# Splitting the last 512-token block of a fused attention/FFN/soft-MoE kernel in two, sharing its regrouping transfers between two queues, and moving one accumulator update

## The chip, the cores and the metric

The kernel runs on one core of a Trainium2 chip. The metric is the device time of the kernel in microseconds (us). A core has TensorE (PE, matrix products; PEld is its loading of stationary operands), VectorE (DVE), ScalarE (ACT) and GpSimd (POOL). SyncE (SP) computes nothing; in this kernel it issues nearly all DMA transfers. Every engine works through its own instructions in order.

## The reference

```python
kv = einsum('bhsd,bhse->bhde', k, v)              # 8 batches, 8 heads, 576 tokens, head size 64
out = einsum('bhsd,bhde->bhse', q, kv)
out = out / sqrt(mean(out*out, -1) + 1e-6) * g_norm        # -> x: 4608 tokens x 512
h = x @ w_in ; g = h * cos(h) ; y = g @ w_out              # w_in 512 x 2048, w_out 2048 x 512
logits = y @ phi                                           # 32 slots (8 experts x 4)
d = softmax of logits over the tokens ; slot_input = d.T @ y
slot_out[e] = relu(slot_input[e] @ w1[e]) @ w2[e]          # w1, w2: 8 x 512 x 1024, 8 x 1024 x 512
result = softmax(logits over the slots) @ slot_out         # 4608 x 512
```

All is float32. `y` is never formed: the kernel folds `w_out` into `phi` (`wp`) for the logits, and accumulates `A = d.T @ g` over the tokens with a running maximum, to multiply it by `w_out` once at the end.

## The kernel before

Tokens come in nine blocks `j` of 512 (`TB`). A block has 16 slots `f`, one for each 128 of the 2048 columns of `w_in`. A slot `(j, f)` runs in this order: `loads` (DMA issues planned for it), `main` (12 matmuls into PSUM tile `h`, of which there are three), `side` (planned work of other stages), `cos_a` (ACT turns `h` into turns, DVE takes the rest, L387), `post`, `cos_b` (ACT cosine, L391), `cos_c` (DVE multiplies, L437, giving `gT`; then a DVE 32x32 transpose into `tr`, L446), and `fin`. Tables name the slot at which each side task runs; a slot number over 15 is in the next block.

The side tasks that matter here:
- `att_out`, `att_xs`, `att_xT`, `att_lo` make the next block's `xt` (split in two parts) from `q` and the block-diagonal `kvA`. `att_out` ends with a small power on POOL (`ri`, L214), which `att_xs` on DVE needs one slot later.
- `load_kv` (L162) loads pair 0 to 3 of a batch in slots 10 to 13; `kv_pair` (L183, tile `kvps`) uses pairs 0 and 1 in slot 14, 2 and 3 in slot 18.
- `nat_load`, `nat_scale`, `nat_bits`, `nat_low`, `nat_store` (L333, L338, L352) convert `w_out` in blocks 3 to 6 and put it into DRAM as `wo_dr`, by way of the tiles that the kv loads use.
- `regroup` (L480): `tr` holds tokens scattered over partitions by the 32x32 transposes; sixteen transfers of 64 KB for each group of four slots bring them into `g` with tokens on partitions. They stand in slots 7 and 8, 9 and 10, 13 and 14, 17 and 18. All are issued by SP, in one queue with every other load; only the last block has every other one on POOL. Blocks 0, half of 1 and half of the last use transposes on PE instead (`gtr`, L462).
- `l_T` and `slot_acc` (slots 21 and 22, which are 5 and 6 of the next block): 16 matmuls `ab<-g,d` (L588), then on DVE at once `A = A*mb + ab` (L591).

The queue of SP (and that of POOL) has eight semaphores, used in turn, so a transfer is issued only after the eighth before it has landed.

When a buffer is free for good, `fill` loads expert weights (33.5 MB in 128 pieces of 256 KB) into it, in the order in which the tail uses them: `kv`, `vr`, `kr` from slot (7,8), `q`, `kvA` from (7,13), `a` at (8,0), `x1` (8 pieces) at (8,2), `T2` at (8,4), then the weight tiles as the last block uses them up. `load_wo2` loads the converted `w_out` (4.2 MB) in slots 1 to 8 of the last block. All others (84 pieces) come behind the last block. `last_product` computes the last slot in two halves. `last_slots`, then `tail`: `first_layer` (L734), `second_layer` (L761), `half_out` (L786, L788) with twelve 768 KB stores.

Of the kernel before, what the change touches and what calls it, by code (L numbers as in the profile page):

```python
# [50 lines left out]
    lT=21,  # L51
# [14 lines left out]
TB, TT, NB, NR = 512, 4, 9, 6  # L66
# [3 lines left out]
def tile_linear_attention__ffn_cos__soft_moe(  # L70
# [70 lines left out]
    def spans(j, t):  # L141
        p, r = divmod(TT * j + t, 9)
        if r == 4:
            return [(0, 64, 2 * p), (64, 64, 2 * p + 1)]
        return [(0, 128, 2 * p + r // 5)]

    def load_q(j, t):
        if j == 0:
            if t == 0:
                first["q"] = g_p.tile([128, TT, 4, 128], F32, tag="g1", name="q")  # L150
            q_t[j, t] = first["q"][:, t]
        else:
            q_t[j, t] = q_p.tile([128, 4, 128], F32, tag=f"q{(TT * j + t) % 3}", name="q")
        nc.sync.dma_start(out=q_t[j, t], in_=qT[TT * j + t])
# [105 lines left out]
    def stage():  # L260
        ta, tb, tc_ = (t_p.tile([128, 2048], F32, tag=f"T{i}", name="st") for i in range(3))
        wi = const.tile([128, 2, 512], F32, tag="l_tok", name="st_m")
        first["sx"] = x_p.tile([128, 2 * TT, 512], F32, tag="x1", name="st_x")
# [3 lines left out]
        ring.extend([None, ta[:, TB * i:TB * (i + 1)], 1] for i in range(3))  # L267
# [92 lines left out]
    def main(j, f, s=slice(0, TB), ps=None):  # L360
        if ps is None:
            ps = ps_m.tile([128, 512], F32, tag="h", name="h")[:, 0:s.stop - s.start]
        w, x = w_t[f], xt_t[j]
        assert all((j, t) in x_done for t in range(TT)) and ("S", f, 0) in done
        n = 0
        for kk in range(KD):
            for a, b in ((0, 0), (0, 1), (1, 0)):
                nc.tensor.matmul(out=ps, lhsT=w[:, a, kk, :], rhs=x[:, b, kk, s],  # L368
# [38 lines left out]
    def last_product(j, f):  # L407
        ss = [slice(0, TB // 2), slice(TB // 2, TB)]
        hs, ts = [], []
        for i, s in enumerate(ss):  # L410
            main(j, f, s, at_bank("h2")[:, 0:TB // 2] if i else None)
            hs.append(h_t.pop((j, f)))
        run(side, j, f)
        for h in hs:
            ts.append(tmp_one()[:, 0:TB // 2])
            turns(ts[-1], h)
            rest(ts[-1], h)
        run(post, j, f)
        g = ring_next(j, f)
        for t in ts:  # L420
            cosine(t)
        for s, h, t in zip(ss, hs, ts):
            nc.vector.tensor_tensor(out=g[:, s], in0=t, in1=h, op=ALU.mult)
        gT_t[j, f] = g
        run(fin, j, f)

    def ring_next(j, f):
        i = next(i for i, r in enumerate(ring) if (r[0] not in gT_t or j == NB - 1)
                 and (not r[2] or j == 0 or j == 1 and f < 10))
        _, g, extra = ring.pop(i)  # L430
        ring.append([(j, f), g, extra])
        return g

    def cos_c(j, f):
# [4 lines left out]
        if not on_pe(j, f):  # L439
            q, o = divmod(f, 4)  # L440
            if o == 0:
                k = 4 * j + q - 5
                tr_t[j, q] = t_p.tile([128, 4 * TT, 4, 32], F32, tag=f"T{k % 3}", name="tr")
            first_o = 2 if (j, q) == (1, 2) else 0
            for i in range(0 if o == first_o else o, o + 1 if o >= first_o else 0):
                nc.vector.transpose(out=tr_t[j, q][:, :, i, :],  # L446
                                    in_=gT_t[j, 4 * q + i].rearrange("p (b t) -> p b t", t=32))

    def g_half(j, h):
        if (j, h) not in g_t:  # L450
            if (j, h) == (1, 0):
                g_t[j, h] = [x.rearrange("p (x f i) -> p x f i", f=8, i=32) for x in
                             (kv_all[:, 0], kv_all[:, 1], kv_all[:, 2], we)]
            else:
                t = g_p.tile([128, TT, 4, 8, 32], F32, tag=f"g{h}", name="g")
                g_t[j, h] = [t[:, i] for i in range(TT)] + [t]
        return g_t[j, h]

    def gtr(j, f):
        ps = at_bank("tr").rearrange("p (t c) -> p t c", c=128)  # L460
        for t in range(TT):
# [4 lines left out]
        if len(g) > TT:  # L466
            copy_on(e, g[TT][:, :, :, f % 8, :], p4)
# [41 lines left out]
    def l_evac(j):  # L509
        t = one_p.tile([128, TB], F32, tag="ls", name="ls")  # L510
# [629 lines left out]
```

## Time and profile before

| | |
|---|---|
| median of 3 runs | 747.95 us (747.94 to 752.03) |
| profiled execution | 751.21 us, of which span 749.4 us |
| PE / PEld busy | 687.2 us (92%) / 490.7 us (65%) |
| DVE / ACT / POOL busy | 500.7 us (67%) / 333.1 us (44%) / 103.9 us (14%) |
| granted TensorE clock, mean | 0.961 of full speed |
| DMA | 135.09 MB, 58.5% of 16 engines on SP's queue |
| chain that ended last | PE 43%, DMA 21%, SP's queue 14%, DVE 12% |

Shares are shares of the span. The chain follows the last instruction back to what released it. A PE that is busy 92% on average can still be waiting in some stretches and held by DMA in others, so the stretches are read apart: the blocks (180 to 600 us), the last block (600 to 660) and the tail.

### The profile page before, as it was taken

The page shows a single profiled execution, that of the slowest core. Times are in us where ns is not written, and L with a number is a line of the kernel's source. Part 1 is how long each engine was busy: PE and PEld are TensorE (multiplying, and loading weights), DVE is VectorE, ACT ScalarE, POOL GpSimd, SP SyncE. Part 2 cuts the span into 40 slices and gives each one's busy share as a digit, 9 for nine tenths or more (in the row PEclk, how much of TensorE's full clock was granted, in tenths as well). Part 3 has the DMA queues.
Part 4 walks back from the last instruction along what each step waited for, and adds up shares of the span by engine and source line. Part 5 has one row for each costly group of instructions (what it writes and reads, how often), then busy time and mean ns, then how long its engine had stood idle before and what let it go on. Part 6 is the DMA issues. An engine that isn't in the chain of part 4 may idle for free.

```text
span 749.4 us, 11987 instructions
## 1 busy us (share of the span) xinstructions
PE 687.2 (92%) x4432; PEld 490.7 (65%) x4432; DVE 500.7 (67%) x884; ACT 333.1 (44%) x600; POOL 103.9 (14%) x121
## 2 busy tenths in 40 slices
PE   6869999999979999879987997899999999999894
PEld 6757777876637776567656765677676775764354
DVE  4986888866638778747874787577877875443143
ACT  3655676545414453425343534354454443441143
POOL 3351121210000111000100010011001102201400
PEclk9888999999989999989998999899999999999996
DMA  9872543121254745556555456545542778999998
GB/s 335 307 243 89 188 150 117 67 85 43 59 135 100 191 136 126 143 162 160 132 143 161 129 137 156 149 125 140 123 100 62 195 196 255 268 333 418 402 406 347
DMA packets 96058, 135.09 MB, mean 180 GB/s; under 512 B 10880, under 2 KB 66304, under 8 KB 95104
## 3 DMA queue, kind: packets, MB, share of 16 engines
q1 hardware_dynamic: 95488, 133.28, 58.5%
q0 software_dynamic: 512, 1.05, 0.5%
q8 instruction: 35, 0.57, 0.3%
q14 instruction: 23, 0.19, 0.1%
HBM read 91.29 MB, written 13.63 MB: 140 GB/s over the span
## 4 chain that ended last, share of the span: by engine, by line
PE 43%; DMA 21%; SPq 14%; DVE 12%; issue 4%; ACT 3%; POOL 0%; DVEq 0%; ACTq 0%; POOLq 0%
PE h L368 25%; SPq L480 12%; DMA ew<-in_w 7%; DMA kv<-in_w_out 6%; PE ab L588 4%; DMA kv<-in_kv 2%; DVE gT L437 2%; DVE tmp L387 2%; ACT tmp L391 2%; DVE tr L446 2%; PE ops L202 2%; PE tr L462 2%; PE xTps L232 2%; PE kvps L183 2%; DMA q<-in_qT 1%
## 5 line engine op out<-in xcount | busy, mean ns | idle before, releaser
L368 PE MATMUL h<-xt,w 128*128 128x512 f32 (+1 forms) x1740 | 424.3, 398 | 9.4 <-DVE gT L437 6.8
L368 PEld LDWEIGHTS h<-xt,w 128*128 128x128 f32 x1740 | 322.1, 190 | 103.0 <-issue 18.3
L391 ACT ACTIVATE tmp<-tmp,hpi 128x512 f32<-128x512 f32 (+1 forms) x145 | 104.3, 721 | 177.6 <-DVE tmp L387 177.5
L437 DVE TENSOR_TENSOR gT<-tmp,h 128x512 f32<-128x512 f32 x135 | 92.6, 686 | 69.6 <-ACT tmp L391 69.2
L214 POOL TENSOR_TENSOR ri<-ss,mhalf 128x8 f32<-128x8 f32 x36 | 59.4, 1654 | 428.7 <-DVE ss L212 428.7
L387 DVE SCALAR_TENSOR_TENSOR tmp<-h,tmp 128x512 f32<-128x512 f32 (+1 forms) x145 | 97.3, 671 | 29.7 <-ACT tmp L384 28.8
L384 ACT ACTIVATE tmp<-h 128x512 int32<-128x512 f32 (+1 forms) x145 | 85.1, 588 | 48.7 <-PE h L368 48.7
L446 DVE STREAM_TRANSPOSE tr<-gT 128x512 f32<-128x512 f32 x112 | 79.4, 711 | 3.8
L588 PE MATMUL ab<-g,d 128*32 128x512 f32 x240 | 39.5, 615 | 6.3 <-DMA g<-tr 5.2
L236 ACT ACTIVATE xt<-xTps,gn 128x512 fp32r<-128x512 f32 x36 | 24.6, 682 | 45.7 <-PE xTps L232 45.7
L202 PE MATMUL ops<-kvA,q 128*128 128x128 f32 (+1 forms) x320 | 38.8, 280 | 0.0
L183 PE MATMUL kvps<-kv 128*64 128x64 f32 x464 | 20.5, 236 | 18.9 <-issue 11.0
L202 PEld LDWEIGHTS ops<-kvA,q 128*128 128x128 f32 (+1 forms) x320 | 34.7, 182 | 3.1 <-issue 1.5
L183 PEld LDWEIGHTS kvps<-kv 128*64 128x64 f32 x464 | 17.2, 146 | 29.0 <-issue 25.4
L245 DVE SCALAR_TENSOR_TENSOR xt<-xTps,gn,xt 128x512 fp32r<-128x512 f32 x36 | 26.6, 739 | 13.9 <-ACT xt L236 13.8
L588 PEld LDWEIGHTS ab<-g,d 128*32 128x32 f32 x240 | 11.6, 112 | 33.3 <-issue 25.8
L311 POOL TENSOR_TENSOR w<-st_m,w 128x512 fp32r<-128x512 f32 x16 | 21.6, 1348 | 78.5 <-ACT w L306 74.5
L209 ACT ACTIVATE sq<-ops 128x512 f32<-128x512 f32 x32 | 19.1, 596 | 27.9 <-PE ops L202 27.7
L211 DVE TENSOR_REDUCE ss<-sq 128x8 f32<-128x512 f32 x32 | 21.8, 680 | 12.6 <-ACT sq L209 12.5
L492 PE MATMUL l<-gT,wp 128*32 128x512 f32 x216 | 28.8, 605 | 0.0
L232 PE MATMUL xTps<-ident,sq 128*128 128x128 f32 x128 | 23.0, 312 | 1.1 <-DVE sq L221 1.1
L221 DVE TENSOR_TENSOR sq<-ops,ri 128x512 f32<-128x512 f32 x32 | 21.5, 678 | 2.4 <-POOL ri L214 2.4
(160 smaller groups left out, 637.7 us busy)
## 6 DMA issues: line engine op xcount, KB each, us to landing
g<-tr SPq DMA_DIRECT2D x432, 64.0 KB, 2.1
kv<-in_kv SPq DMA_DIRECT2D x29, 512.0 KB, 5.3
ew<-in_w SPq DMA_DIRECT2D x27, 512.0 KB, 12.5
q<-in_qT SPq DMA_DIRECT2D x36, 256.0 KB, 3.1
out<-ot SPq DMA_DIRECT2D x12, 768.0 KB, 6.6
rw<-in_w_in SPq DMA_DIRECT2D x16, 512.0 KB, 5.8
kv<-in_w_out SPq DMA_DIRECT2D x16, 512.0 KB, 3.6
st<-in_w_outT SPq DMA_DIRECT2D x15, 512.0 KB, 3.8
```

Of the source, the lines that this page charges most:

```text
L183: nc.tensor.matmul(out=ps[h], lhsT=t[:, 0, r, h], rhs=t[:, 1, r, h], start=(r == 0), stop=False)
L202: nc.tensor.matmul(out=ps[p0:p0 + n, pr * 128:(pr + 1) * 128], lhsT=q_t[j, t][:, pr, p0:p0 + n], rhs=kvbd[b % 2][:, pr, :], start=True, st ...
L214: nc.gpsimd.tensor_tensor(out=ri[:, :, 0], in0=ss, in1=mhalf, op=ALU.pow)
L232: nc.tensor.transpose(ps[:, kk * 128:(kk + 1) * 128], xs[:, kk * 128:(kk + 1) * 128], ident)
L368: nc.tensor.matmul(out=ps, lhsT=w[:, a, kk, :], rhs=x[:, b, kk, s], start=(n == 0), stop=(n == 3 * KD - 1))
L384: nc.scalar.activation(out=t.bitcast(I32), in_=ps, func=AF.Copy, bias=0.25, scale=INV_2PI)
L387: nc.vector.scalar_tensor_tensor(out=t, in0=ps, scalar=INV_2PI, in1=t.bitcast(I32), op0=ALU.mult, op1=ALU.subtract)
L391: nc.scalar.activation(out=t, in_=t, func=AF.Sin, bias=hpi, scale=TWO_PI)
L437: nc.vector.tensor_tensor(out=g, in0=fr, in1=h_t.pop((j, f)), op=ALU.mult)
L446: nc.vector.transpose(out=tr_t[j, q][:, :, i, :], in_=gT_t[j, 4 * q + i].rearrange("p (b t) -> p b t", t=32))
L480: (nc.gpsimd if j == NB - 1 and b % 2 else nc.sync).dma_start(out=dst[32 * b:32 * b + 32, :, x, a:a + 4, :].rearrange("p t f i -> p t (f i)"),
L588: nc.tensor.matmul(out=ps[32 * c:32 * c + 32, :], lhsT=d[:, t, :], rhs=gs[c // 2][t][:, (c % 2) * 512:(c % 2) * 512 + 512], start=(t == 0) ...
```

## The change

1. The nine blocks of 512 become eight of 512 and two of 256 (`SIZES`; `SMALL` is 8, the first of the small ones). Every tile of a block takes its size from the list. The small blocks use eight slots to one regrouping group (1 KB runs where there were 512 bytes), one `g` tile for both halves, halves of the old `gT` ring, and halves of one `tmp`. The last block's `xt` lies in `T2`. The regrouping of a small block stands in slots 9 and 10, 17 and 18; the last one's second half is still transposed on PE. `last_product` is gone.
2. `ring` and `tmp` are two tiles each, so that one of each can be freed early. The fills move: `x1` to (8,1), `gt1` and `tmp1` at (8,5), `q` and `kvA` to (8,12), `a` to (8,15), `x0` at (9,0), `load_wo2` to block 9, `T1` at (9,6), `g0` at (9,12), `T0` at (9,14). Before the end of the last block 68 pieces are issued instead of 44.
3. Every other regrouping transfer is issued by POOL in all blocks.
4. The update of `A` becomes `slot_add`, planned in `fin` of the slot instead of directly behind the matmuls.

```diff
-TB, TT, NB, NR = 512, 4, 9, 6
+TB = 512
+SIZES = (512,) * 8 + (256,) * 2
...
+SMALL = SIZES.index(256)
...
         for x in xs:
             for b in range(4):
-                (nc.gpsimd if j == NB - 1 and b % 2 else nc.sync).dma_start(
-                    out=dst[32 * b:32 * b + 32, :, x, a:a + 4, :].rearrange("p t f i -> p t (f i)"),
+                (nc.gpsimd if b % 2 else nc.sync).dma_start(
+                    out=dst[32 * b:32 * b + 32, :, x, a:a + n, :].rearrange("p t f i -> p t (f i)"),
...
+        ab_t[j] = (ps, mb)
+
+    def slot_add(j):
+        if j == NB - 1:
+            return
+        ps, mb = ab_t.pop(j)
         if j:
             nc.vector.scalar_tensor_tensor(out=A, in0=A, scalar=mb[:, 3:4], in1=ps,
                                            op0=ALU.mult, op1=ALU.add)
...
+        lT, sa = (PLAN["F"][j] if j < 2 else (22, 23) if j == NB - 1 else (23, 26) if j >= SMALL
+                  else (PLAN["lT"], PLAN["sa"]))
         at2(j, lT, l_T, j)
         at2(j, sa, slot_acc, j)
+        end2(j, sa, slot_add, j)
...
+    ld_at(8, 1, fill, x_p, "x1", 8)
+    ld_at(8, 5, fill, gt_p, "gt1", 3)
+    ld_at(8, 5, fill, const, "tmp1", 1)
...
+    ld_at(9, 0, fill, x_p, "x0", 8)
     for n in range(8):
-        ld_at(8, n + 1, load_wo2, n)
-    ld_at(8, 4, fill, t_p, "T2", 4)
+        ld_at(9, n + 1, load_wo2, n)
+    ld_at(9, 6, fill, t_p, "T1", 4)
+    ld_at(9, 12, fill, g_p, "g0", 8)
+    ld_at(9, 14, fill, t_p, "T0", 4)
```

SP's order in block 3, from the issue behind slot 6 on (`kv<-in_w_out` is nat_load, `wo_dr<-kv` nat_store, `kv<-in_kv` load_kv), before:

```order
L333 DMA kv<-in_w_out 128x1024
L480 DMA g<-tr 32x4x128 x8
L352 DMA wo_dr<-kv 4x32x512
L333 DMA kv<-in_w_out 128x1024
L480 DMA g<-tr 32x4x128 x16
L154 DMA q<-in_qT 128x512
L480 DMA g<-tr 32x4x128 x8
L162 DMA kv<-in_kv 128x1024
L352 DMA wo_dr<-kv 4x32x512
L162 DMA kv<-in_kv 128x1024
```

and now:

```order
L340 DMA kv<-in_w_out 128x1024
L476 DMA g<-tr 32x4x128 x4
L359 DMA wo_dr<-kv 4x32x512
L340 DMA kv<-in_w_out 128x1024
L476 DMA g<-tr 32x4x128 x8
L160 DMA q<-in_qT 128x512
L476 DMA g<-tr 32x4x128 x4
L168 DMA kv<-in_kv 128x1024
L359 DMA wo_dr<-kv 4x32x512
L168 DMA kv<-in_kv 128x1024
```

The order is the same; between the slot-6 issue and the second pair's load stand 16 regrouping transfers instead of 32.

DVE in slots 5 to 7 of the same block, around the update of `A` (L591 before), before:

```order
L446 STREAM_TRANSPOSE tr<-gT 128x16x32
L300 SCALAR_TENSOR_TENSOR kv<-kv 128x512
L591 SCALAR_TENSOR_TENSOR A<-A,mb,ab 128x512
L245 SCALAR_TENSOR_TENSOR xt<-xTps,gn,xt 128x4x128
L387 SCALAR_TENSOR_TENSOR tmp<-h,tmp 128x512
L221 TENSOR_TENSOR sq<-ops,ri 128x512
L437 TENSOR_TENSOR gT<-tmp,h 128x512
L446 STREAM_TRANSPOSE tr<-gT 128x16x32
L387 SCALAR_TENSOR_TENSOR tmp<-h,tmp 128x512
```

and now (L594):

```order
L437 STREAM_TRANSPOSE tr<-gT 128x16x32
L307 SCALAR_TENSOR_TENSOR kv<-kv 128x512
L252 SCALAR_TENSOR_TENSOR xt<-xTps,gn,xt 128x4x128
L393 SCALAR_TENSOR_TENSOR tmp<-h,tmp 128x512
L227 TENSOR_TENSOR sq<-ops,ri 128x512
L427 TENSOR_TENSOR gT<-tmp,h 128x512
L437 STREAM_TRANSPOSE tr<-gT 128x16x32
L594 SCALAR_TENSOR_TENSOR A<-A,mb,ab 128x512
L393 SCALAR_TENSOR_TENSOR tmp<-h,tmp 128x512
```

The update, which waits for the matmuls on PE, now stands behind the whole of slot 6 on DVE.

SP from the last group of block 7 on (`ew` are expert weights, `wo` is load_wo2), before, where that is in the last block:

```order
L480 DMA g<-tr 32x4x128 x8
L643 DMA ew<-in_w 128x512 x2
L480 DMA g<-tr 32x4x128 x8
L945 DMA wo_5244<-wo_dr 128x1024
L480 DMA g<-tr 32x4x128 x8
L643 DMA ew<-in_w 128x1024
L643 DMA ew<-in_w 128x2048
```

and now, in the first small block:

```order
L476 DMA g<-tr 32x4x128 x12
L646 DMA ew<-in_w 128x512
L646 DMA ew<-in_w 128x2048
L646 DMA ew<-in_w 128x1536
L476 DMA g<-tr 32x4x128 x4
L646 DMA ew<-in_w 128x512
L646 DMA ew<-in_w 128x1024
L646 DMA ew<-in_w 128x512
L476 DMA g<-tr 32x2x256 x8
```

The eight pieces of `x1` (4096 columns) now stand ahead of the last four transfers of block 7 on SP; the other eight of that group are on POOL.

## Rows read from the trace of the kernel before

**Rows 1.** Windows: stretch, engines' busy us, then granted clock, DMA share, GB/s

```profile
194.50:204.50 10.00, 10.00 (x57) 7.58 (x54) 6.39 (x17) 5.25 (x9) 1.64 (x1) 1.00 0.44 93
...
323.60:340.00 16.40, 16.40 (x112) 12.95 (x114) 10.03 (x17) 5.87 (x9) 0.00 (x0) 0.85 0.51 132
...
598.20:656.70 58.50, 57.51 (x285) 40.50 (x282) 32.93 (x55) 27.34 (x44) 8.97 (x16) 1.00 0.85 237
...
680.40:715.90 35.50, 33.00 (x280) 11.00 (x279) 9.06 (x12) 4.59 (x7) 9.77 (x36) 1.00 1.03 408
```

**Rows 2.** Waits of the whole span: total us, times, longest

```profile
DVE A L591 <- PE ab L588: 15.1, 7, 10.0
...
PE kvps L183 <- issue: 11.0, 2, 5.6
...
PE h L368 <- DVE gT L437: 6.8, 9, 1.2
```

**Rows 3.** Timeline of PE around kv_pair: start, us, instruction, [idle before]

```profile
251.45 0.64 PE L183 MATMUL kvps<-kv 128*64 128x64 f32 x16
...
252.54 11.16 PE L368 MATMUL h<-xt,w 128*128 128x512 f32 x48
...
323.57 1.12 PE L183 MATMUL kvps<-kv 128*64 128x64 f32 x16 [5.49 <-DMA kv<-in_kv]
...
325.61 12.48 PE L368 MATMUL h<-xt,w 128*128 128x512 f32 x48
```

**Rows 4.** Timeline of SP's queue: start, us, issues

```profile
194.25 10.39 SPq L480 DMA_DIRECT2D g<-tr  x16
...
286.07 6.40 SPq L480 DMA_DIRECT2D g<-tr  x8
...
293.69 13.56 SPq L480 DMA_DIRECT2D g<-tr  x16
...
313.14 0.52 SPq L162 DMA_DIRECT2D kv<-in_kv  x1
...
314.39 0.40 SPq L162 DMA_DIRECT2D kv<-in_kv  x1
```

**Rows 5.** Timeline of PE around slot_acc, of block 1 and of block 2

```profile
211.24 1.03 PE L588 MATMUL ab<-kv,d 128*32 128x512 f32 x4
...
218.03 1.03 PE L588 MATMUL ab<-g,d 128*32 128x512 f32 x1 [4.14 <-DMA g<-tr]
...
223.87 5.74 PE L368 MATMUL h<-xt,w 128*128 128x512 f32 x24
...
282.12 4.72 PE L588 MATMUL ab<-g,d 128*32 128x512 f32 x32 [0.27 <-DVE d L564]
```

**Rows 6.** Timeline of POOL: its first regrouping issues in the last block

```profile
629.75 3.99 POOL L480 DMA_DIRECT2D g<-tr  x7 [37.78 <-DMA ew<-in_w]
636.29 0.56 POOL L480 DMA_DIRECT2D g<-tr  x1 [2.55 <-DMA g<-tr]
```

**Rows 7.** L480 on POOL: from issue to landing of its transfers

```profile
DMA to landing us min/median/max: 5.8/6.7/7.2
```

**Rows 8.** Groups by form, those of 256 columns: busy us, mean ns | idle before

```profile
L368 PE MATMUL h<-xt,w 128*128 128x256 f32 x24 | 3.1, 287 | 0.0
...
L391 ACT ACTIVATE tmp<-tmp,hpi 128x256 f32<-128x256 f32 x2 | 0.9, 500 | 0.2 <-DVE tmp L387 0.2
...
L387 DVE SCALAR_TENSOR_TENSOR tmp<-h,tmp 128x256 f32<-128x256 f32 x2 | 0.8, 420 | 1.6 <-ACT tmp L384 1.6
```

**Rows 9.** Timeline of PE in the tail

```profile
668.54 2.16 PE L608 MATMUL ab<-g,d 128*32 128x128 f32 x64 [0.58 <-DVE d L564]
...
705.78 0.59 PE L761 MATMUL eo<-kv,hT 128*32 128x256 f32 x2
...
715.88 1.21 PE L772 MATMUL sel<-so,sel 128*96 128x256 f32 x4
...
720.29 1.50 PE L761 MATMUL eo<-ew,hT 128*32 128x256 f32 x24
```

More of the change, by code (lines that the diff above doesn't have):

```diff
@@ L65 @@
 )
-TB, TT, NB, NR = 512, 4, 9, 6
+TB = 512
+SIZES = (512,) * 8 + (256,) * 2
+NB = len(SIZES)
+TT = [n // 128 for n in SIZES]
+T0 = [sum(TT[:j]) for j in range(NB)]
+NT = sum(TT)
+SMALL = SIZES.index(256)
 @with_exitstack
@@ L357, in on_pe, with main @@
         return j == 0 or j == 1 and f < NF // 2 or j == NB - 1 and f >= NF // 2
-    def main(j, f, s=slice(0, TB), ps=None):
-        if ps is None:
-            ps = ps_m.tile([128, 512], F32, tag="h", name="h")[:, 0:s.stop - s.start]
+    def main(j, f):
+        ps = ps_m.tile([128, 512], F32, tag="h", name="h")[:, 0:SIZES[j]]
         w, x = w_t[f], xt_t[j]
-        assert all((j, t) in x_done for t in range(TT)) and ("S", f, 0) in done
+        assert all((j, t) in x_done for t in range(TT[j])) and ("S", f, 0) in done
         n = 0
@@ L405, in cos_b @@
         cosine(fr_t[j, f])
[L407 to L425, printed above, removed]
     def ring_next(j, f):
+        if (j, f) == (SMALL, 0):
+            ring[:] = [[r[0], r[1][:, a:a + 256], 2 * r[3], r[3]] for k in range(2) for r in ring
+                       if r[3] == k and r[2] != 1 for a in (0, 256)]
         i = next(i for i, r in enumerate(ring) if (r[0] not in gT_t or j == NB - 1)
[L429 to L432, printed above, removed]
+                 and (not r[2] or r[2] == 1 and (j == 0 or j == 1 and f < 10) or r[2] == 2 and (j, f) < (SMALL, 2)))
+        r = ring.pop(i)
+        ring.append([(j, f)] + r[1:])
+        return r[1]
     def cos_c(j, f):
@@ L555, in l_exp @@
         sc_t[j] = mb
+    ab_t = {}
     def l_T(j):
@@ L604, in ab @@
             ps = abs_[o % 2]
-            for t in range(TT):
+            for t in range(TT[-1]):
                 for c in range(4):
@@ L678, in c_split @@
         if j not in cs_t:
-            w = w_p.tile([128, 3, 3, 3 * NS], F32, tag=f"w{10 + j // 3}", name="cs")
-            cs_t.update((j + x, w[:, x]) for x in range(3))
+            w = x_p.tile([128, 12, 3, 3 * NS], F32, tag="x1", name="cs")
+            cs_t.update((x, w[:, x]) for x in range(12))
         cs = cs_t[j]
@@ L813, in tail @@
         second_layer(1, 1)
-        half = {1: (select(1), two(g_p, "g1") + two(g_p, "g0") + two(gt_p, "gt"))}
+        half = {1: (select(1), two(g_p, "g0") + [gt_p.tile([128, 1536], F32, tag=f"gt{i}", name="ot") for i in (1, 0)]
+                    + two(g_p, "g1"))}
         for u in range(2):
@@ L921, in tile_linear_attention__ffn_cos__soft_moe @@
             ao, dx, xt, dl = PLAN["A"][n]
-        for t in range(TT):
-            i = TT * j + t + 3
-            if i < TT * NB:
-                ld_at(n, ao[t] + 1, load_q, *divmod(i, TT))
+        for t in range(TT[j]):
+            i = T0[j] + t + 3
+            if i < NT:
+                jj = max(x for x in range(NB) if T0[x] <= i)
+                ld_at(n, ao[t] + 1, load_q, jj, i - T0[jj])
             at2(n, ao[t], att_out, j, t)
```

154 lines of the change are left out of this document (80 added, 74 removed).

## The prediction

> **What bounds the kernel now.** I read the windows by stage first. PE runs nearly without a break in the blocks, and from the last block on the DMA engines are the fuller resource: their share is 0.85 while the last block is computed and 1.03 at 408 GB/s in the tail [rows 1]. So two questions: what holds PE in the blocks, and what holds DMA in the tail.
>
> The list of waits answers the first. PE's dearest waits are not for another engine but for a load: the second pair of `kv_pair` waits 5.49 us in block 3 [rows 3], and two more, of up to 5.6 us, 11.0 together, are booked as "issue" in blocks 4 and 5 [rows 2]; the timeline puts them at the same matmul. The load is not slow because of its size. It is issued at 314.39 [rows 4], some nine microseconds before PE resumes at 323.57 [rows 3], because SP stands behind regrouping transfers: from 286.07 SP issues 8 and then 16 and 8 more of them, and comes to the kv loads at 313.14 [rows 4]. The price goes on after the wait: from the late pair to the end of the next 48 matmuls PE takes 338.09 - 323.57 = 14.52 us, against 263.70 - 251.45 = 12.25 for the same work in block 2 [rows 3]; the granted clock in that stretch is 0.85 [rows 1], a mixture of the two levels, after an idle PE. One wait thus costs 5.5 + 2.3 us.
>
> The same queue holds the accumulation of block 1: `ab` begins at 211.24, stops 4.14 us for a regrouping transfer, and the next main product begins at 223.87, 12.6 us later; the same 32 matmuls take 4.72 us in block 2 [rows 5]. In the tail the second layer's first half of experts 4 to 7 begins at 705.78 and ends at 715.88, 10.1 us for 64 matmuls of which 24 take 1.50 us elsewhere, that is 4.0 us [rows 9]: the weights come late.
>
> **POOL takes half of the regrouping.** SP issues 16 transfers in 10.39 us, 0.65 each [rows 4]. Between the issue behind slot 6 and the second kv load stand 32, now 16: that load can be issued up to 16 x 0.65 = 10.4 us earlier, and 5.5 are needed. It also waits for the conversion of `w_out` to leave its buffer, but that conversion's own load stands behind the same transfers and moves up too. The DMA engines have room: with SP issuing nothing but regrouping their share is 0.44 [rows 1], so two queues ask for about 0.88. I take the three waits as gone: 11.0 + 5.5 + 3 x 2.3 = 23.4 us. Bounds: nothing gained if the load lands as late as now, 23.4 at most.
>
> A rule speaks against this. The Trainium skill, "DMA: Bandwidth & Descriptors", section "Issuing engines are not separate DMA queues", says that transfers started from several engines share the same 16 DMA engines, and that starting them from more than one saves only sequencer time, usually small beside the transfer. By the rule's "usually" the term would be near 0; by the row it is 23.4, since the sequencer needs 0.65 us for a transfer and the engines are only 0.44 busy meanwhile.
>
> Block 1's `ab`: SP's 32 transfers ahead of it become 16, 10 us less for a 4 us wait. 12.6 - 4.7 = 7.9; I take 7.5 (bounds 4.1, the wait alone, and 7.9).
>
> POOL has its own price. It issued seven transfers in 3.99 us (0.57 each), and the eighth waited 2.55 us, until the first had landed [rows 6], 6.7 us after its issue [rows 7]. That was with DMA full; at that pace 16 transfers need about 0.85 us each, 14 us, in blocks of over 60 us. Behind them on POOL stands `ri`, for which DVE's `att_xs` waits. Eight transfers (4.6 us at 0.57) begin when `ab` ends, in slot 6, and the next `ri` belongs to slot 8: hidden, 0.
>
> **The update of `A` moves.** DVE waited 15.1 us for `ab` in seven places, 10.0 of them in block 1 [rows 2], with slot 6's rest queued behind. Now the slot's cosine runs under the matmuls, and what is late next is the next slot's rest, by less. PE gets back part of its 6.8 us of waits for `gT` [rows 2]; bounds 0 and 6.8, I take 2. Against it: while PE waited for kv, DVE and ACT caught up. Without those breaks new short waits of PE may come; bounds 0 and 8 (those 6.8 once more and a little), I take 3, about half.
>
> Blocks together: -23.4 - 7.5 - 2 + 3 = -29.9 us.
>
> **Two small blocks.** 24 products of 256 columns take 3.1 us [rows 8], so a slot 1.55; 32 slots 49.6. Before, 15 slots of 12 x 11.16/48 = 2.79 us [rows 3] and the split one of 3.1 made 45.0. So +4.6. One more accumulation with two token tiles instead of four, half of 4.72: +2.4. Further logits, max and transposes for one more block, less the narrower PE transposes: +1, my estimate from the counts of instructions, of the length of one such group. DVE and ACT alternate in a slot: rest 420 ns, cosine 500 ns [rows 8], multiply and transpose each about as long as the rest: 1.76 us against 1.55 on PE, in 24 slots up to 5 us, of which accumulations and attention on PE hide a good half: +2 (bounds 0 and 9, if fixed costs and the softmax's short steps show). Together +10.
>
> The last group of block 7 must land before `ab` in slot (8,6), and before ACT may write `xt` into `T2` at (8,5). Its last four on SP stand behind `x1`, 2.1 MB, 5.1 us at 408 GB/s; its eight on POOL need 8 x 0.57 + 6.7 = 11.3 us. Slots of 1.55 us and a few others give about 11 to 14 us: +2, bounds 0 and 6.
>
> **The tail.** `last_slots` has half the matmuls; 64 take 2.16 us [rows 9], 64 of 128 go: -2.2. Maximum, exponential and copies of half size: -1 (0 to 2). The late second layer: 24 more pieces, 6.3 MB, are issued before the last block ends, 15.4 us at 408 GB/s. Room for them: 0.15 of 58.5 us is 8.8 us [rows 1], and the longer small blocks add about 12. So they fit and 10.1 - 4.0 = 6.1 us go (bounds 0 and 6.1). The rest, from 715.88 [rows 9] to the span's end 749.4, is 33.5 us for 9.4 MB of output, 23 us at 408 GB/s, partly shared with weights now: -2 (0 to 6). Together -11.3.
>
> **Sum.** -29.9 + 10 + 2 - 11.3 = -29.2 on the profiled execution's 751.2 us gives 722.0; that execution is 3.3 us above the median of 747.95, so 718.8 by the median. I say 718.5.
>
> **Rivals.**
> - The kv waits close only in part, because two queues fill the DMA engines in bursts and each transfer lands later (6.7 us on POOL when full [rows 7]). For it: the kv load took nine microseconds though the DMA engines were about half busy (0.51 in the stretch behind it [rows 1]). With 10 of 23.4 us gained, 732.
> - The end costs more: small slots paced by DVE and ACT (+17 instead of +10), the last group of block 7 late (+6), weights not earlier (-5 instead of -11.3): 17 more, 736. Against it: DMA room worked out above.
> - No effect: the 16 engines, not the issue, set the pace. Then only -2 and +3 remain in the blocks, and the end's +0.7: 750 by the median. Against it: share 0.44 [rows 1].
> - Slower: POOL's issues are held. Place: eight issues between the end of `ab` in slot 6 and `ri` of slot 8. From there to `att_xs` are about 16 us in block 3, less 1.6 for `ri`: above some 1.8 us an issue, against 0.57 measured, DVE and then PE wait. At 3 us they wait 10 us in each of five blocks: 718.5 + 50 = 768. The Trainium skill, "SBUF — State Buffer", section "SBUF: two separate sides", gives such a mechanism: DVE in a two-port mode keeps POOL from writing its descriptors. No run here shows it; the only POOL issues [rows 6] lie where the conversion of `w_out` does not run.
> - Better: DMA never falls behind, outputs follow at once, no new DVE waits: 706.
>
> **How the numbers follow.** Forecast 0.58 (its own range 709 to 728), partly closed 0.13, dear end 0.13, no effect 0.05, slower 0.06, better 0.05. The range 704 to 738 takes in all but the "no effect" and "slower" cases and the edges of the dear end. About 1% (7.5 us) is what a measurement of this kernel can tell from no change; below 740.5 lie the forecast, better and most of the two dear cases: faster 0.88, same 0.06, slower 0.06.
>
> **What would show it.** Right: no wait over 1 us at `kvps` in blocks 3 to 5; `ab` of block 1 near 4.7 us; SP's kv loads before slot 12; blocks 8 and 9 about 10 us longer than block 8 was; the second layer without DMA waits. Wrong: `att_xs` waiting for `ri`, PE waiting for `g<-tr` in block 8, a DMA share at 1.0 already in blocks 3 to 6, or small slots near 2 us.

## The result, and the profile after

The changed kernel takes 724.21 us (median of four executions, 718.57 to 726.98) against 749.99 us for the kernel before on the same chip: a ratio of 0.964, 95% interval 0.955 to 0.972. The prediction was 718.5 us with a range of 704 to 738. The profiled execution took 718.57 us (span 716.6); it is the quickest of its four, and the experiments show what probably separates them.

The time went as follows. Stages are cut at PE rows: where the accumulation `ab` of blocks 0 and 6 begins (slot 6 of blocks 1 and 7), the end of the last `main`, the first product of the first expert layer (`eh`), the first `sel`. The column in the middle is experiment e1, explained below: the kernel before with nothing but POOL's half of the regrouping.

| stage, us | before | e1 | after |
|---|---|---|---|
| start to `ab` of block 0 | 190.5 | 190.4 | 190.1 |
| to `ab` of block 6 | 375.6 | 340.1 | 340.3 |
| to the end of the last `main` | 93.7 | 92.9 | 108.8 |
| last softmax, slot inputs | 20.6 | 20.7 | 16.0 |
| first layer, half of the second | 35.5 | 27.9 | 27.9 |
| output | 33.5 | 32.5 | 33.4 |
| span | 749.4 | 704.5 | 716.6 |

The changed kernel is better than before by 33 us of span in these two profiles, and worse than one of its own parts by 12. Windows of it, columns as in [rows 1]:

```profile
274.20:339.50 65.30, 63.50 (x390) 45.91 (x390) 51.63 (x96) 29.98 (x49) 24.38 (x36) 1.00 0.64 170
...
530.50:639.30 108.80, 101.56 (x706) 79.72 (x703) 70.27 (x157) 50.16 (x103) 35.45 (x59) 0.98 0.78 227
...
655.30:683.20 27.90, 27.88 (x279) 10.35 (x278) 8.98 (x11) 4.59 (x7) 9.76 (x36) 1.00 1.03 399
```

From `ab` of block 2 to `ab` of block 3 it takes 65.3 us, PE busy in 63.5 of them at a granted clock of 1.00; before it took 356.51 - 282.12 = 74.4. The DMA share is 0.64, so the 16 engines are not full.

PE at `kv_pair` in block 3, to be held against [rows 3]: the long wait is gone, and the 48 products behind it are back at the full clock.

```profile
308.69 0.64 PE L189 MATMUL kvps<-kv 128*64 128x64 f32 x16
...
309.78 11.16 PE L374 MATMUL h<-xt,w 128*128 128x512 f32 x48
```

SP's queue ahead of it, to be held against [rows 4]: 4, 8 and 4 transfers stand where 8, 16 and 8 stood. The second load leaves at 297.75, 10.9 us before PE comes to the pair at 308.69; before, 318.08 - 314.39 = 3.7 us (323.57 less the wait of 5.49). The lead grew by 7.2 us where 5.5 were missing.

```profile
278.33 2.86 SPq L476 DMA_DIRECT2D g<-tr  x4
...
282.94 9.88 SPq L476 DMA_DIRECT2D g<-tr  x8
...
293.50 2.54 SPq L476 DMA_DIRECT2D g<-tr  x4
...
296.15 0.52 SPq L168 DMA_DIRECT2D kv<-in_kv  x1
...
297.75 0.33 SPq L168 DMA_DIRECT2D kv<-in_kv  x1
```

POOL at the place that the prediction named, between the end of `ab` in slot 6 and the next `ri`: seven issues, a hold of 1.01 us, the eighth issue, then an idle engine until `ss` is there. Here `ri` waits for its input, and not for the issues ahead of it.

```profile
278.71 4.04 POOL L476 DMA_DIRECT2D g<-tr  x7 [1.88 <-PE ab L585]
283.76 0.55 POOL L476 DMA_DIRECT2D g<-tr  x1 [1.01 <-issue]
287.76 1.67 POOL L220 TENSOR_TENSOR ri<-ss,mhalf 128x8 f32<-128x8 f32 x1 [3.46 <-DVE ss L218]
```

Block 1's `ab`, [rows 5] before, runs through; the next `main` starts 215.88 - 210.87 = 5.0 us after it begins, where it was 12.6.

```profile
210.87 0.62 PE L585 MATMUL ab<-kv,d 128*32 128x512 f32 x2
...
215.88 0.97 PE L374 MATMUL h<-xt,w 128*128 128x512 f32 x3
```

The two small blocks, PE. Two long waits are new, for `ld` of the softmax and for `gT` right behind a softmax step. `ab` of block 7 starts without a wait. The first half of the second layer, [rows 9] before, now runs from 676.22 to 683.24 with no wait for weights.

```profile
577.49 0.46 PE L559 MATMUL ldT<-ident,ld 64*128 64x64 f32 x4 [2.43 <-DVE ld L542]
...
581.64 5.09 PE L585 MATMUL ab<-g,d 128*32 128x512 f32 x32
...
600.95 6.65 PE L374 MATMUL h<-xt,w 128*128 128x256 f32 x48
...
617.41 2.93 PE L374 MATMUL h<-xt,w 128*128 128x256 f32 x12 [3.24 <-DVE gT L427]
...
676.22 3.64 PE L764 MATMUL eo<-ew,hT 128*32 128x512 f32 x32
...
683.24 1.23 PE L775 MATMUL sel<-so,sel 128*96 128x256 f32 x4
```

DVE in four small slots without other work. The rest of one slot begins 1.79 us after that of the slot before (602.68 - 600.89, 604.47 - 602.68), and each multiply has waited 0.58 us for ACT's cosine: DVE goes through rest, wait, multiply, transpose in strict order.

```profile
600.89 0.39 DVE L393 SCALAR_TENSOR_TENSOR tmp<-h,tmp 128x256 f32<-128x256 f32 x1
...
602.68 0.39 DVE L393 SCALAR_TENSOR_TENSOR tmp<-h,tmp 128x256 f32<-128x256 f32 x1
603.64 0.42 DVE L427 TENSOR_TENSOR gT<-tmp,h 128x256 f32<-128x256 f32 x1 [0.58 <-ACT tmp L397]
604.10 0.45 DVE L437 STREAM_TRANSPOSE tr<-gT 128x256 f32<-128x256 f32 x1
604.47 0.38 DVE L393 SCALAR_TENSOR_TENSOR tmp<-h,tmp 128x256 f32<-128x256 f32 x1
```

### The profile page after: what moved, and what is told of

The parts are those of the page before. It is cut to its first block, busy times and chain, and to the rows that moved or that the text cites. A ratio compares the mean times of both kernels' runs of the same rounds, so it can differ in the third digit from the quotient of the medians.

```text
span 716.6 us, 12698 instructions
## 1 busy us (share of the span) xinstructions
PE 673.7 (94%) x4578; PEld 492.2 (69%) x4578; DVE 509.6 (71%) x941; ACT 339.0 (47%) x635; POOL 225.7 (32%) x337
## 4 chain that ended last, share of the span: by engine, by line
PE 58%; DVE 18%; DMA 10%; ACT 7%; issue 4%; SPq 1%; POOL 0%; DVEq 0%; ACTq 0%; POOLq 0%
PE h L374 35%; DMA kv<-in_w_out 4%; PE ab L585 4%; DVE gT L427 4%; ACT tmp L397 3%; DVE tmp L393 3%; PE ops L208 3%; DVE tr L437 2%; PE l L488 2%; PE kvps L189 2%; PE eh L737 2%; DVE ss L217 2%; PE tr L457 2%; PE xTps L239 2%; PE l L497 1%
## 5 line engine op out<-in xcount | busy, mean ns | idle before, releaser
L374 PEld LDWEIGHTS h<-xt,w 128*128 128x128 f32 x1920 | 332.7, 190 | 99.3 <-issue 18.3
L397 ACT ACTIVATE tmp<-tmp,hpi 128x512 f32<-128x512 f32 (+1 forms) x160 | 108.8, 681 | 172.5 <-DVE tmp L393 172.4
L476 POOL DMA_DIRECT2D g<-tr x232 | 128.3, 556 | 115.4 <-DVE tr L437 45.6
L427 DVE TENSOR_TENSOR gT<-tmp,h 128x512 f32<-128x512 f32 (+1 forms) x152 | 95.8, 630 | 77.8 <-ACT tmp L397 77.4
L390 ACT ACTIVATE tmp<-h 128x512 int32<-128x512 f32 (+1 forms) x160 | 87.5, 547 | 54.8 <-PE h L374 53.8
L437 DVE STREAM_TRANSPOSE tr<-gT 128x512 f32<-128x512 f32 (+1 forms) x128 | 84.4, 661 | 6.0 <-DMA g<-tr 0.5
L318 POOL TENSOR_TENSOR w<-st_m,w 128x512 fp32r<-128x512 f32 x16 | 23.7, 1479 | 77.4 <-ACT w L313 77.4
L488 PE MATMUL l<-gT,wp 128*32 128x512 f32 (+1 forms) x248 | 30.2, 559 | 0.0
L239 PE MATMUL xTps<-ident,sq 128*128 128x128 f32 x128 | 20.5, 287 | 0.4 <-DVE sq L227 0.4
```

Of the source, the lines that this page charges most:

```text
L390: nc.scalar.activation(out=t.bitcast(I32), in_=ps, func=AF.Copy, bias=0.25, scale=INV_2PI)
L397: nc.scalar.activation(out=t, in_=t, func=AF.Sin, bias=hpi, scale=TWO_PI)
L427: nc.vector.tensor_tensor(out=g, in0=fr, in1=h_t.pop((j, f)), op=ALU.mult)
L437: nc.vector.transpose(out=tr_t[j, q][:, :, i, :], in_=gT_t[j, n * q + i].rearrange("p (b t) -> p b t", t=32))
L476: (nc.gpsimd if b % 2 else nc.sync).dma_start(out=dst[32 * b:32 * b + 32, :, x, a:a + n, :].rearrange("p t f i -> p t (f i)"), in_=src[32 ...
L488: nc.tensor.matmul(out=l_t[j][32 * o:32 * o + 32, :], lhsT=wp[:, f, :], rhs=gT_t.pop((j, f)), start=(c == 0), stop=(c == (2 if j == NB - 1 ...
```

## The experiments

Each was run in four executions beside the kernel before on the same chip; e3 had ten. Parts are numbered as in the text: 1 the two small blocks, 2 the half-size buffers and the loads moved with them, 3 POOL's half of the regrouping, 4 the update of `A`.

### e1: part 3 alone

```diff
-                (nc.gpsimd if j == NB - 1 and b % 2 else nc.sync).dma_start(
+                (nc.gpsimd if b % 2 else nc.sync).dma_start(
```

> The kernel before with one edit: every second regrouping transfer is issued by POOL in all blocks (part 3 alone). My theory (the three long waits at `kv_pair` are the place of the kv loads in SP's queue behind 16 transfers of 0.65 us each): no wait over 1 us at `kvps` in blocks 3 to 5, the `ab` of block 1 at 4.7 to 6 us where it was 13 us with its 4.14 us wait, the starts of `ab` in blocks 3, 4 and 5 earlier by 16 to 18, 26 and 35 us, the end at 715 to 722 us against about 749 (ratio 0.955 to 0.965). The last block keeps its 59 us. Rival, the DMA engines set the pace whoever issues: 745 to 752 us, the kv loads leave SP earlier but land as late. Rival, POOL is held by its issues: 760 us or more, `att_xs` waits for `ri`.

708.53 us (705.92 to 712.32), ratio 0.944, interval 0.939 to 0.948: 42 us less than before, quicker than the 715 to 722 expected, and below every execution of the changed kernel. Its windows from `ab` of block 6 on, and SP's last loads:

```profile
530.50:623.40 92.90, 92.36 (x483) 66.47 (x480) 59.40 (x98) 41.44 (x66) 31.41 (x51) 1.00 0.86 243
...
644.10:672.00 27.90, 27.89 (x279) 10.33 (x278) 9.00 (x11) 4.59 (x7) 9.70 (x36) 1.00 1.01 389
```

```profile
607.81 40.15 SPq L643 DMA_DIRECT2D ew<-in_w  x26
```

The waits go as forecast. What was not expected is the stage 644.10 to 672.00: it fell from 35.5 to 27.9 us, although no weight load was moved to another slot. The last series of weight loads starts at 607.81, 15.7 us before the last `main` ends at 623.5 (before: 659.35, at the end of that product). So the late second layer looked like the same queue once more; e11 tests it.

### e2: the changed kernel without part 3

```diff
-                (nc.gpsimd if b % 2 else nc.sync).dma_start(
+                (nc.gpsimd if j == NB - 1 and b % 2 else nc.sync).dma_start(
```

> The changed kernel with part 3 undone (POOL issues transfers of the regrouping in the last block alone, as before). My theory: the three waits at `kvps` come back (11 to 12.5 us of row at clock 0.85, as in rows 3), and the time is 745 to 752 us, that of the kernel before, since the small blocks cost at the start of the end what the shorter tail gives (14.6 of loss in blocks 8 and 9 by the trace of the changed kernel, 12 of gain behind them). If the two small blocks are a gain in themselves: 735 to 743 us. If the regrouping of the small blocks needs POOL too: over 755 us.

774.69 us (772.77 to 775.81), ratio 1.031, interval 1.028 to 1.034: parts 1, 2 and 4 alone make the kernel 24 us slower, which is the last of the three expected cases and not my theory. `ab` of block 6 starts at 567.90 (before 566.07), so the loss lies behind it: `ab` of block 7 waits for its last transfers, and the second layer for its weights, though parts 1 and 2 issue 24 loads earlier.

```profile
627.14 5.13 PE L585 MATMUL ab<-g,d 128*32 128x512 f32 x26 [5.80 <-DMA g<-tr]
...
727.92 3.19 PE L764 MATMUL eo<-ew,hT 128*32 128x512 f32 x25 [1.51 <-DMA ew<-in_w]
```

Loads that were placed earlier in the program gained nothing here, since they stood in a queue that was behind.

### e7: parts 3 and 4 without the small blocks

The diff is that of e1, and `slot_add` of the change run in `fin` of the slot of `ab`.

> The kernel before with parts 3 and 4 and without the two small blocks and their buffers: what the changed kernel is without parts 1 and 2. By my sum parts 1 and 2 are worth +0.7 us net (+12 in the blocks, -11.3 behind them), so 722 us against 724 of the changed kernel, ratio to before 0.955 to 0.965. By the trace of the changed kernel the last blocks cost 14.6 and the tail gives 12: 2 to 3 us less than the changed kernel, 718 to 722. If the small blocks pay (the tail cannot take the weights earlier without them): 728 to 735.

709.76 us (707.71 to 710.78), ratio 0.943, interval 0.940 to 0.945, below all three expected cases. Without parts 1 and 2 the kernel takes 14.5 us less than the changed one (0.943 against 0.964 of the kernel before on its chip). The products and everything else of PE from slot 15 of block 7 to the last `main`, in e7 and in the changed kernel; the second row of each kernel counts `main` alone:

```profile
566.81:627.50 60.69, 60.16 (x310) 43.70 (x309) 34.83 (x58) 28.27 (x45) 13.35 (x25) 1.00 0.93 277
...
566.81:627.50 60.69, 49.46 (x216) 38.35 (x216) 23.14 (x34) 10.09 (x17) 1.00 0.93 277
```

```profile
559.99:639.30 79.31, 72.07 (x558) 59.71 (x555) 49.32 (x124) 37.91 (x84) 20.61 (x35) 0.98 0.78 240
...
559.99:639.30 79.31, 56.25 (x396) 50.91 (x396) 28.02 (x66) 12.20 (x32) 0.98 0.78 240
```

The stretch is 18.6 us longer. `main` costs 6.8 us more (56.25 - 49.46), PE's idle time 6.7 us more (7.24 against 0.53). The other 5.1 are mostly attention work that stood ahead of the stretch before (some 3 us) and the additional accumulation (`ab`, 7.35 us against 5.04).

### e3 and e4: part 4 alone, and the change without it

```diff
+        end2(j, sa, slot_add, j)     # e3, on the kernel before
-        end2(j, sa, slot_add, j)     # e4, on the changed kernel
+        at2(j, sa, slot_add, j)
```

> The kernel before with the update of `A` run behind the cosine of its slot (part 4 alone). Forecast: -2 us, 746 to 749 us, ratio 0.995 to 1.0; by the trace of the changed kernel the wait `DVE A<-PE ab` (15.1 us of DVE in the kernel before) falls out of the list of waits. Bounds of the prediction: 0 and -6.8 us. If the first product behind `ab` then waits less for DVE's `gT`, its row (PE h<-DVE gT, 6.8 us in all) falls; if not, the time is the same.

> The changed kernel with part 4 undone (the update of `A` stands directly behind `ab` again). Forecast: +2 us on the changed kernel (724 by its median), bounds 0 and +6.8; the wait `DVE A<-PE ab` comes back with some 15 us of DVE. If the update is worth nothing: the same time within 0.5%.

e3: 751.05 us, ratio 1.0008, interval 0.998 to 1.003. e4: 724.16 us (717.81 to 726.11), the changed kernel's 724.21. The edit is worth nothing that can be measured. In e3's list of waits DVE's wait for `ab` fell from 15.1 to 5.5 us, and PE's wait for `gT`, which was to fall with it, stayed at 6.8 us in nine places, as in [rows 2]:

```profile
PE h L368 <- DVE gT L437: 6.8, 9, 1.2
...
DVE A L599 <- PE ab L588: 5.5, 1, 5.5
```

e4's profile shows something else, which has to do with the small blocks and not with its edit, since e9 shows it too. SP comes to the last series of weight loads at 640.82 instead of 633.08, and the second layer waits again: from 675.35 to `sel` at 689.80, with short waits for its pieces, as in the kernel before.

```profile
640.82 26.48 SPq L646 DMA_DIRECT2D ew<-in_w  x23
```

```profile
675.35 1.06 PE L764 MATMUL eo<-ew,hT 128*32 128x512 f32 x6
...
683.50 1.70 PE L764 MATMUL eo<-kv,hT 128*32 128x256 f32 x25 [0.67 <-DMA kv<-in_w2h]
...
689.80 1.20 PE L775 MATMUL sel<-so,sel 128*96 128x256 f32 x4
```

### e5: kv loads on POOL, regrouping on SP

```diff
-        nc.sync.dma_start(out=t, in_=kv[b, pr])
+        (nc.gpsimd if b >= 5 else nc.sync).dma_start(out=t, in_=kv[b, pr])
```

> The kernel before with one edit: the kv loads of batches 5 to 7 are issued by POOL, and the regrouping stays on SP. It tells a place in a queue from the transfers' own pace. If the three waits of 11 to 12.5 us (rows 3) are the place in SP's queue: they shrink below 1 us each, -15 to -23 us, 726 to 734 us, while the `ab` of block 1 keeps its 4.14 us wait. If 16 transfers of 64 KB fill the DMA engines: the loads leave POOL at their slot and still land late, the waits stay at 5 us or more each, 742 to 750 us.

736.25 us (735.48 to 742.59, the slowest profiled), ratio 0.980, interval 0.976 to 0.985. The regrouping transfers are all still there and still on one queue; the kv load alone has another, and `kvps` no longer waits. That settles what the wait was: a place in SP's queue, not the pace of the transfers. The gain is smaller than 23 us because the next load in SP's queue becomes the late one. SP is busy with 32 transfers until 344.42; the load of `w_out` behind them is issued at 344.58; ACT, which begins its conversion, waits 3.32 us for it; DVE, which stands behind ACT, copies `d` only at 353.31; `ab` waits for `d` (3.42, 3.13 and 3.00 us in the three blocks).

```profile
317.37 27.05 SPq L480 DMA_DIRECT2D g<-tr  x32
344.58 0.47 SPq L333 DMA_DIRECT2D kv<-in_w_out  x1
```

```profile
348.54 0.66 ACT L338 ACTIVATE kv<-kv 128x512 f32<-128x512 f32 x1 [3.32 <-DMA kv<-in_w_out]
```

```profile
319.82 0.64 PE L183 MATMUL kvps<-kv 128*64 128x64 f32 x16
...
353.65 6.56 PE L588 MATMUL ab<-g,d 128*32 128x512 f32 x32 [3.42 <-DVE d L564]
```

### e10: every fourth transfer on POOL

```diff
-                (nc.gpsimd if j == NB - 1 and b % 2 else nc.sync).dma_start(
+                (nc.gpsimd if b == 1 or j == NB - 1 and b % 2 else nc.sync).dma_start(
```

> The kernel before with every fourth regrouping transfer issued by POOL instead of every second (the last block as before). Of the 32 transfers of 0.65 us that stood before the second kv load 8 move: the load leaves SP 5.2 us earlier, and 5.49 us of wait were to be closed. If the wait is the place in the queue and nothing else: a wait of some 0.3 us or none at `kvps` in blocks 3 to 5, and nearly the whole gain of the half-and-half split in these blocks; block 1's `ab` gains only about 5 of 8 us and the second layer keeps part of its late weights, so 712 to 722 us against 708.5 for the half-and-half split. If the gain goes with the number moved: half of 42 us, 729 us.

718.16 us (712.49 to 720.05), ratio 0.954, interval 0.950 to 0.958. Half as many moved transfers bring 34 of the 42 us, so the gain does not go with the number. But the waits did not close: 2.77, 3.19 and 2.23 us are left. The load leaves at 302.44, only 7.5 us before PE comes to the pair (312.76 - 2.77 = 309.99). The lead grew by 3.8 us and not by 5.2, since PE reaches the pair sooner as well, and the load took 10.2 us to land where it took 9.0 before (7.7 in the changed kernel). The second layer, which was to stay late in part, runs through in 7.0 us (678.82 to 685.84).

```profile
312.76 0.69 PE L183 MATMUL kvps<-kv 128*64 128x64 f32 x16 [2.77 <-issue]
```

### e11: POOL's half in blocks 7 and 8 only

```diff
-                (nc.gpsimd if j == NB - 1 and b % 2 else nc.sync).dma_start(
+                (nc.gpsimd if j >= NB - 2 and b % 2 else nc.sync).dma_start(
```

> The kernel before with every second regrouping transfer issued by POOL in the last two 512-token blocks only (7 and 8). Blocks 1 to 6 stay as before, so the three waits and block 1's `ab` stay. In the run with the split in all blocks the first half of the second layer takes 3.6 us instead of 10.1 and the end moves 9.3 us closer to the start of block 6's `ab`, although no weight load was moved to another slot. If SP's queue in block 7 held those weights: -6 to -9 us, 741 to 744 us, `eo` without DMA waits. If the shorter blocks before gave the weights their room (or the DMA engines, with the share at 1.03, decide): 748 to 752 us, the waits on `in_w2h` as before.

741.51 us (739.89 to 742.22), ratio 0.987, interval 0.985 to 0.989: -10 us with all waits of the earlier blocks in place (5.53, 5.55 and 4.62 us at `kvps`). The second layer runs through in 705.66 - 698.63 = 7.0 us:

```profile
698.63 3.64 PE L761 MATMUL eo<-ew,hT 128*32 128x512 f32 x32
702.09 1.91 PE L761 MATMUL eo<-kv,hT 128*32 128x256 f32 x32
...
705.66 1.23 PE L772 MATMUL sel<-so,sel 128*96 128x256 f32 x4
```

So without the small blocks the late weights are cured by taking half of block 7's regrouping out of SP's queue. With the small blocks that is not always enough (e4, e9).

### e6: all regrouping on POOL

```diff
-                (nc.gpsimd if b % 2 else nc.sync).dma_start(
+                nc.gpsimd.dma_start(
```

> The changed kernel with all regrouping transfers issued by POOL instead of every second one. It measures what POOL's issues cost, and tests the rival that held issues make the kernel slower. In the changed kernel 232 issues take 128 us of POOL (0.55 us each); 464 would take 256 us, of a POOL that is 32 % busy. My theory: the group of 8 issues of 0.55 us stands in front of `ri` for 4.4 us in place of 2.2, inside a slot of 3.4 us and its neighbour: 0 to +6 us on the changed kernel, 724 to 730. If POOL's issues are held (over 1.8 us each at any time): `sq` waits for `ri` by over 5 us in all, 740 us or more. If half-and-half was not needed because SP is now the free queue: below 724.

765.58 us (762.79 to 767.62), ratio 1.017, interval 1.014 to 1.020: 41 us slower than the changed kernel, and my theory was wrong; the case "POOL's issues are held" came. POOL is held in the middle of a group of 16, and everything behind follows in a chain, to be read from engine to engine: POOL waits 4.03 us to issue, `ri` comes after it, DVE has waited 6.90 us for `ri`, PE 3.66 us for DVE.

```profile
381.06 4.04 POOL L476 DMA_DIRECT2D g<-tr  x7 [0.77 <-issue]
389.12 0.55 POOL L476 DMA_DIRECT2D g<-tr  x1 [4.03 <-issue]
...
392.39 1.67 POOL L220 TENSOR_TENSOR ri<-ss,mhalf 128x8 f32<-128x8 f32 x1
```

```profile
394.09 0.69 DVE L227 TENSOR_TENSOR sq<-ops,ri 128x512 f32<-128x512 f32 x1 [6.90 <-POOL ri L220]
```

```profile
394.93 1.09 PE L239 MATMUL xTps<-ident,sq 128*128 128x128 f32 x4 [3.66 <-DVE sq L227]
```

This is the rival "POOL's issues are held", at the double load. In the changed kernel that wait for `ri` is 2.4 us in all, as before; here 43.3.

What holds an issue can be read from the landings. Seven issues go out from 381.06 on; the first of them lands 7.8 us after its issue, at 388.9, and the eighth is issued at 389.12. In 39 of POOL's waits in this run, 57 us together, the issue comes 0.31 us after the seventh transfer before it has landed. So POOL's queue has at most seven transfers under way in these rows, and not eight as its eight semaphores would let expect. Seven issues take 4 us; a transfer that lands later than that holds the next issue. Why some land after 7.8 us, with a median of 2.7, no run shows.

### e8 and e9: what makes the small blocks dear

e8 sets the exponential of blocks 7 and 8 one slot later, and the transpose and `ab` of block 7 two slots later. e9 replaces their exponentials by a copy, so four table loads of ACT fall away and the weights of these tokens are other numbers.

```diff
-            (at2, late2, end2)[how](j, NF + lx, l_exp, j)                              # e8
+            (at2, late2, end2)[how](j, NF + lx + (j >= SMALL - 1), l_exp, j)
-                  else (PLAN["lT"], PLAN["sa"]))
+                  else (23, 24) if j == SMALL - 1 else (PLAN["lT"], PLAN["sa"]))
-        nc.scalar.activation(out=ld, in_=ps, func=AF.Exp, ...)                         # e9
+        ex = AF.Identity if j in (SMALL - 1, SMALL) else AF.Exp
+        nc.scalar.activation(out=ld, in_=ps, func=ex, ...)
```

> The changed kernel with the softmax steps that fall into the two small blocks set to later slots: the exponential of blocks 7 and 8 one slot later, the transpose of block 7's weights from slot 5 of block 8 to slot 7, its `ab` from slot 6 to slot 8. In the changed kernel PE waits 2.43 us for `ld` in block 8 (577.5 us) and 3.24 us for `gT` in block 9 (617.4 us), behind two table loads of 1.28 us each. If these waits set the end: -3 to -5 us. If from 615 us on the transfers set it (DMA share 1.02 to 1.04 there, 340 to 410 GB/s): the products of the first layer end earlier, the second layer waits for its weights instead, and the end moves by less than 1 us.

> The changed kernel, with the exponentials of the softmax of blocks 7 and 8 replaced by a copy (Identity, with the same bias and the same sum), so that ACT needs no table load there: four loads of 1.28 us each fall out of the two small blocks, and the weights of these two blocks' tokens are other numbers. Nothing else changes. If the table loads make the small blocks dear: the PE waits of 2.43 us (for `ld`) and 3.24 us (for `gT`) fall below 1 us each, the stretch of the small blocks loses 4 to 6 us, 718 to 720 us by the median. If the step of DVE and ACT in each small slot (1.76 us for 1.66 us of PE) makes them dear and the softmax only comes on top of it: PE waits elsewhere for `gT`, the stretch loses less than 2 us.

e8: 728.20 us (724.69 to 733.73), not better. The waits moved to other places: 1.07 and 2.66 us for `gT`, 1.75 for `d`. e9: 723.76 us (721.28 to 725.18), the same as the changed kernel. The two waits shrank to 1.15 and 0.54 us, and the stretch from slot 15 of block 7 to the last `main` took 640.2 - 563.34 = 76.9 us instead of 79.3, a gain of 2.4: a little over what the second theory allowed, and well under the 4 to 6 of the first. In its place small waits for `gT` stand all along the blocks. So the table loads are the smaller part; that a slot for which DVE and ACT need 1.79 us has no slack to take them up is argued from these rows and not shown by a run of its own.

```profile
579.56 0.46 PE L560 MATMUL ldT<-ident,ld 64*128 64x64 f32 x4 [1.15 <-DVE ld L543]
...
618.21 1.70 PE L374 MATMUL h<-xt,w 128*128 128x256 f32 x12 [0.54 <-DVE gT L427]
```

e9's profile also has the late second layer of e4 (last series of loads from SP at 639.44). Two profiled executions with small blocks and POOL's half show it, two (the changed kernel and e8) don't, and it costs 6 to 7 us (12.9 from 676.92 to 689.84 in e9, 14.45 from 675.35 to 689.80 in e4, 7.0 in the changed kernel). In e8 SP is as late (640.55), and PE comes to the second layer late as well (683.10). From the start of that series to the end of the span it is 83.5 us in the changed kernel, 82.1 in e4, 83.7 in e9, 82.4 in e8 and 82.9 in e2: in these profiles with small blocks the end goes with the moment at which SP comes to that series. The 6 to 8 us by which SP is late are about the width of the changed kernel's own four times, 718.57 to 726.98. That they differ by this is likely, but not shown: of its executions only the quickest was profiled. Nor was it settled what holds SP there.

## Why the prediction was right, and where it was not

The time lies in the range and on the side that was forecast, and the mechanism that was named carries it. But that the number came so close is partly luck, since the sum holds two errors that cancel: part 3 is worth more than the forecast gave it, and parts 1 and 2, which were to break even, cost 12 to 15 us.

- **kv waits, -23.4: right, and over its bound of 23.4.** Between `ab` of block 2 and `ab` of block 5 the kernel gained (503.88 - 282.12) - (468.69 - 274.17) = 27.2 us; e1 gained 26.7. Of the 27.2, 19.0 are less idle time of PE (forecast 16.5) and 8.2 shorter rows of PE, at a granted clock of 1.00 instead of 0.95 (forecast 6.9). That the price of a wait includes the slow clock behind it holds: the 48 products are back from 12.48 to 11.16 us. e5 shows the cause by itself. The rival "closes only in part" is what a quarter on POOL gives (e10); half was enough, with 7.2 us more lead for a wait of 5.5.
- **Lost cover, +3: not seen.** These blocks gained 27.2 us where 23.4 + 2 - 3 = 22.4 were forecast; PE's waits for `gT` in them did not grow (3.2 us in the changed kernel, 3.4 in e1, 4.8 before).
- **Block 1's `ab`, -7.5: right,** 7.6 us measured (12.6 to 5.0).
- **Update of `A`, -2: wrong, 0.** The failed step is "PE gets back part of its 6.8 us of waits for `gT`". The edit did cut DVE's wait, from 15.1 to 5.5 us; but those waits of PE were not behind it (e3). A wait of DVE that PE did not follow cost nothing here.
- **POOL's price, 0: right, with less room than claimed.** The sum counted 0.85 us an issue as bearable on average. e6 shows that the average is not what matters: a group of 16 is held in the middle, with `ri` behind it. In the changed kernel 11 issues are held in this way, 14.9 us in all and 2.6 at most, and nothing waits for that.
- **Small blocks, +12 with the last group of block 7: mis-sized, 15.9** (108.8 - 92.9 against e1). The step that failed is the slot time and its cover. `main` was put at 1.55 us a slot from a pair of 3.1 us; 48 products that stand together take 6.65 us, 1.66 a slot, and 1.68 where a slot stands alone: +6.8 instead of +4.6. The pace of DVE and ACT was right at 1.76 (1.79 measured), but the part of which "accumulations and attention on PE hide a good half", +2, became 6.7 us more of idle PE, most of it in two waits around the softmax (2.43 and 3.24 us). The accumulation (2.26 us for 16 matmuls, at 628.07, forecast 2.4) was as forecast; the wait for block 7's last group, +2, did not come (none at `ab`).
- **The end of the softmax, -3.2: 4.7 gained** (20.7 to 16.0).
- **Late second layer, -6.1: the time came, from another part.** 7.6 us were gained, but e1 and e11 gain them without the small blocks and e2 does not gain them with all of the moved loads. The step that failed is "So they fit and 10.1 - 4.0 = 6.1 us go": it counted bytes against DMA room, and the loads were held by their place in SP's queue, the very cause that the first part of the prediction had named for kv. In e4 and e9 they are late even so, for a reason that is open.
- **Output, -2: 0** (33.5 to 33.4).

Put together by the chip, by medians of runs on several chips: part 3 -42 us, part 4 none, parts 1 and 2 +14.5 on top of it, the change -26. The sum had +0.7 for parts 1 and 2 (12 less 11.3); of the 11.3 only the softmax's 4.7 is theirs. By the traces their cost is 15.9 - 4.7 + 0.9 of output = 12.1 us.

The rule that was weighed, the Trainium skill, "DMA: Bandwidth & Descriptors", section "Issuing engines are not separate DMA queues", says that starting DMAs from several engines saves only the sequencer's time, usually small beside the transfer. That the engines are shared agrees with the traces: a 64 KB transfer lands after 3.5 to 3.6 us on either queue, where it took 2.1 us with SP alone (e2). That the saving is small does not: here it is 42 of 750 us, since loads that PE waits for stand behind up to 32 issues of 0.65 us. The measurement decides. The other page that was cited, the Trainium skill, "SBUF — State Buffer", section "SBUF: two separate sides", gives DVE as a cause for held POOL writes. e6's holds end with a landing on POOL's own queue; whether DVE makes some of these landings late no run here tells.

```profile
g<-tr SPq DMA_DIRECT2D x232, 64.0 KB, 3.6
g<-tr POOLq DMA_DIRECT2D x232, 64.0 KB, 3.5
```

The best kernels of this study are e1 and e7, which cannot be told apart (0.944 and 0.943 of the time before); e1 is one line of the change.

## What to carry to other kernels

When a load is late, read the issuing queue ahead of it before its size: if an engine waits for one transfer and the queue is issuing others, another queue can be worth the whole wait, unless the next load of the old queue becomes the late one (e5: 16 of 23 us), and moving loads to an earlier slot of the same queue may be worth nothing (e2). Make the parts of a change stand alone before adding them up, since a total can be right while one part pays for another. Before halving a tile, see whether the engines that follow the product also halve: here a slot of PE went from 2.79 to 1.66 us, and one of DVE and ACT from 2.80 (DVE, 602.68 to 605.48 in the kernel before) to 1.79.

## What the runs showed of the hardware that was not expected

- POOL's issues of 64 KB transfers were held until 0.31 us after the seventh transfer before had landed: 11 times in the changed kernel, with groups of eight (14.9 us in all), 39 times in e6, with groups of 16 (57 us, up to 5.1 each). The compute instructions behind them on POOL wait as well. Not every group is held (one of 16 went out in 9.28 us).
- With two queues issuing, each transfer lands later (3.5 us instead of 2.1) while the kernel is faster: the time to land is not what the kernel pays for.
- 24 products of 256 columns end 3.1 us after they start, 48 only after 6.65: it may be that the pace of the engines that empty PSUM shows there in PE's rows without an idle gap being listed; no run tells this apart from a cost of PE's own.
